# One instruction order from a table, and a ninth group on seven products, in a fused attention and feed-forward kernel

## The chip, the cores and the metric

The kernel runs on one core of a Trainium2 chip. The metric is the device time of one execution in microseconds (us). A core has engines that each run their instructions in order: TensorE (PE, the matrix engine), VectorE (DVE), ScalarE (ACT), GpSimd (POOL) and SyncE (SP, which mostly starts DMAs). They wait for each other by semaphores. Matrix products land in PSUM banks, which DVE and ACT read.

## What is computed

```python
B, H, S, D = 8, 8, 512, 64        # x: (B, H, S, D), state: (B, H, 32, D)
scale = 1.0 / np.sqrt(D)
scores = scale * x @ state^T ; a = softmax(scores)
xread = a @ state                  # tokens read from the states
scores2 = scale * state @ x^T ; a2 = softmax(scores2)
sread = a2 @ x                     # states read from the tokens
attn = concat([xread, sread], axis=2)          # 544 rows for each b and h
x = attn.transpose(0, 2, 1, 3).reshape(4352, 512)
h = x @ w_in                       # 512 -> 2048
out = (h * clip(h + 3, 0, 6) / 6) @ w_out      # 2048 -> 512, float32
```

## The kernel before

The rows of tokens of a batch are the attention weights times the states, so the kernel multiplies the states into w_in first: for every batch it makes W' = states x w_in (`wprime`, L660), in four chunks c of 512 of the 2048 inner columns, and takes the attention weights `aT` straight into the feed-forward product. Work goes in 144 steps n: 16 for each of the 8 batches, 16 for the rows of states of all batches. A step has a first product (`first`, `first_grouped`: `ps_h<-aT,wp`), a gate on ACT (L1204, L1374) and DVE (L1206, L1377), a split of the result in a high and a low half of 16 bits, `g_hi` and `g_lo`, and a second product (`second`, `second_grouped`) that adds into accumulators `acc0` to `acc3`. A product of two split operands is three terms: hi hi, hi lo, lo hi (`product`, L1133 is its matmul). The split is near (ACT makes hi, DVE lo, L422 and L423) or far (ACT hi, DVE minus hi, and an accumulating DMA of POOL adds the number itself, L449, L450, L452).

Batches from `HALF_FROM` = 2 on work in 16-bit floats; before them the operands are 32 bits wide. A batch with a number in `SEVEN` is grouped: its 512 tokens are two groups q of 256 with 8 steps each, and a step has 256 inner columns. Bit q of `SEVEN[b]` says that group q makes its second product by a scheme of Strassen's kind: 2 x 2 blocks with seven products of 128-blocks in place of eight. For that DVE makes two sums of gated blocks (L1215: one of 256 elements, one of 384), the weights have mixed forms T (`mixed_weights`), and the seven results are added up at the end of the group (L1280). A batch with 0 there has 16 steps of 512 tokens and 128 inner columns.

The order of the work is a plan. Each operation is recorded by `add` (through `T` for PE, `V` DVE, `S_` ACT, `P_` POOL, `Q` for DMAs of SP) with an engine, an expected cost, a rank, what it depends on and which buffers (slots) it takes. `order` places them by expected times: the first 566 of a table `OPENING`, then always an operation that could start soonest, by rank among those that start about equally soon. Tables of steps (`PLANS`, `FETCH`, `PAIRED_AT`, `MIXED_AT`, `CONVERTED`, `WPRIME_AT`) and others (`FAR`, `BEHIND`) set the ranks. `issue` runs the operations in that order, so the order of every engine is fixed when the program is built; in the opening it puts idle matmuls into expected gaps of PE (L1834).

Side work for a later batch is laid between the steps: DMAs that load x and the state, transposes of x on DVE (L806), scores of the states over the tokens and their softmax (`states`: row maximum L997, exps L1001), a move of those weights into another layout by a DVE transpose and 16 DMAs on SP (`weights_moved`, L1060), the states' read (`tokens_read`: PE L1089, with a scaling L1098 and a copy L1064 of the result on DVE), and the weights' split forms (L531, `converted`, `w_in_paired`).

The rows of states come last. Their two accumulators of 128 x 512 are emptied at the end of `second`: one by DVE (L1445), the last by ACT (L1442), and each is stored by a DMA of SP (L1460).

Of the kernel before, what the change touches and what calls it, by code (L numbers as in the profile page):

```python
# [46 lines left out]
SEVEN = [0, 0, 0, 0, 3, 3, 3, 3]  # L47
PAIRED = 3
WPRIME_AT = [1, -3, -2, -3]
BY_PAIRS = False  # L50
PAIRED_AT = [44, 30, 49, 30]
MIXED_AT = [44, 42, 50, 44, 48, 55, 48, 65]
CONVERTED = [19, 21, 29, 29, 30, 33, 33, 30, 31, 39, 36, 37, 34, 44, 37, 43]
EXTRA_FROM = 70
PLANS = [[1, -6, 16, 12, 5, -4, 4, 7], [-4, 5, 2, 14, 8, 5, 6, 8], [-12, -6, -11, 10, 5, 4, -5, 7], [-5, 4, 10, 9, 6, -10, 27, 9], [-9, -1, 9, 20, -1, -3, -5, 2], [-6, 2, -1, 24, 5, 13, -5, 21], [-5, 0, 12, 10, 6, 2, 18, 6]]
FETCH = [[4, 4], [19, 16], [26, 26], [39, 42], [61, 50], [69, 73], [95, 74]]
STATES_AT = 25
MAXIMA_AT = 25
WEIGHTS_AT = 20
FAR = [0, 0, 1, 1, 3, 4, 4, 1]  # L60
BEHIND = [1.0, 0.75, 1.75]
ADDED = 2.3
SLOWER = 1.18
EVICTED = (2, 3, 4, 5, 6, 7)
OPENING_ROWS = 566
SQUEEZE = 0.3
URGED = [34, 2.0]
PLAIN = 1
STATES = 121
# [3 lines left out]
OPENING = """  # L73
# [16 lines left out]
class Plan:  # L90
# [51 lines left out]
    def order(self):  # L142
        opening = [self.told[int(n)] for n in OPENING.split()[:OPENING_ROWS] if self.told[int(n)] is not None]
        n_ops = len(self.ops)
        held = {}
# [3 lines left out]
        self.home = {}  # L149
        waits = [len(op[4]) for op in self.ops]  # L150
        heirs = [[] for _ in range(n_ops)]
        for n, op in enumerate(self.ops):
            for d in op[4]:
                heirs[d].append(n)
        ready = [0.0] * n_ops
        open_ops = {e: set() for e in "TVSPQ"}
        for n in range(n_ops):
            if not waits[n]:
                open_ops[self.ops[n][0]].add(n)
# [4 lines left out]
        row, self.start, self.took = [], [0.0] * n_ops, [0.0] * n_ops  # L164
        placed = set()
        while len(row) < n_ops:
            best = None
            while opening and opening[0] in placed:
                opening.pop(0)
            told = opening[0] if opening and not waits[opening[0]] else None  # L170
            if told is not None:
                e = self.ops[told][0]
                t = max(clock[e], ready[told])
                for x in sorted(self.extra & open_ops[e], key=lambda x: (self.ops[x][2], x)) if len(row) > EXTRA_FROM else ():
                    at = max(clock[e], ready[x])
                    room = all(slot in held or any(f[0] <= at for f in free[slot[0]]) for slot in self.ops[x][5])
                    if room and at + self.ops[x][1] <= t + (1.0 if e == "Q" else SQUEEZE):
                        told = x
                        break
            more = opening and told is None and any(self.extra & s for s in open_ops.values())  # L180
            for e, numbers in open_ops.items():
                if told is not None:
                    numbers = {told} & numbers
                elif more:
                    numbers = self.extra & numbers
                can = []
                for n in numbers:
                    need = {}
                    for slot in self.ops[n][5]:
                        if slot not in held:  # L190
                            need[slot[0]] = need.get(slot[0], 0) + 1
                    if any(len(free[tag]) < k for tag, k in need.items()):
                        continue
                    t = max(clock[e], ready[n])
                    for tag, k in need.items():
                        t = max(t, sorted(free[tag])[k - 1][0])
                    if e == "Q":
                        t = max(t, min(flying))
                    can.append((t, self.ops[n][2], n))
                if not can:  # L200
                    continue
                soon = min(can)[0]
                t, rank, n = min(
                    (c for c in can if c[0] <= soon + (0.8 if c[1] <= 0.0 else 0.3)),
                    key=lambda c: c[1:],
                )
                if best is None or soon < best[0]:
                    best = (soon, t, n, e)
            if best is None:
                stuck = [self.ops[n][3].__name__ for s in open_ops.values() for n in s]  # L210
                raise RuntimeError(f"the plan is stuck: {stuck[:20]}; held: {[s for s in held if left[s]]}")
            _, t, n, e = best
            _, cost, _, _, _, slots, size = self.ops[n]
            if e == "T" and t < self.WARM:
                cost *= 2
            self.took[n] = cost
            new = [slot for slot in slots if slot not in held]
            for tag in dict.fromkeys(slot[0] for slot in new):
# [1646 lines left out]
```

## Time and profile before

| | us |
|---|---|
| median of 3 runs | 607.17 |
| lowest, highest | 606.9, 610.45 |
| the profiled execution's own time | 607.82 |
| its span, first to last instruction | 605.9 |
| PE, DVE, ACT, POOL busy | 594.2, 482.6, 387.4, 82.0 |

The granted clock of TensorE is 1.0 of full speed, its 2.4 GHz level, in practically the whole span. Busy time counts an engine's instructions; the span is one execution on the chip. An engine that is busy for less than the span waits somewhere, but only a wait of the engine that sets the end costs time. A matmul of 256 columns is one instruction, and so is one of 512; a step's time on PE is that of its matmuls together.

### The profile page before, as it was taken

The numbers are of one execution on the slowest core, as the hardware profiler recorded it, in microseconds if no ns is written. First come the engines' busy times: TensorE is split into PE (matmuls) and PEld (weight loads), VectorE is DVE, ScalarE is ACT, GpSimd is POOL, SyncE is SP. The second block draws the span as 40 slices with busy tenths as digits, with TensorE's granted clock in tenths as the row PEclk, the third lists the DMA queues.
The fourth block names the chain that finished last, engine by engine and source line by source line (L and its number), as shares of the span: only waits on it lengthen the run. The fifth ranks groups of instructions, "written<-read, shape, count | busy, mean of one in ns | idle before, by whom it ended". The sixth has DMA issues, their size and how long they took to land.

```text
span 605.9 us, 12698 instructions
## 1 busy us (share of the span) xinstructions
PE 594.2 (98%) x5041; PEld 424.6 (70%) x5041; DVE 482.6 (80%) x870; ACT 387.4 (64%) x633; POOL 82.0 (14%) x102
## 2 busy tenths in 40 slices
PE   8999999999999999999999999999999999999996
PEld 6577778778554444444468877888778878888763
DVE  6989997588899985598689887987879888788432
ACT  5988888887576765574565656475645566464432
POOL 2000000113231212220102011212121210000000
PEclk9999999999999999999999999999999999999999
DMA  8999152978691477993368594935497451211101
GB/s 288 376 196 326 48 127 36 204 141 141 117 244 18 75 95 110 185 173 48 43 123 134 77 142 52 160 48 67 85 141 116 83 63 18 51 16 16 70 2 35
DMA packets 148987, 67.99 MB, mean 112 GB/s; under 512 B 124864, under 2 KB 137792, under 8 KB 148800
## 3 DMA queue, kind: packets, MB, share of 16 engines
q1 hardware_dynamic: 135824, 45.95, 32.0%
q0 software_dynamic: 12960, 21.17, 25.5%
q8 instruction: 39, 0.64, 0.5%
q14 instruction: 20, 0.16, 0.1%
q10 hardware_dynamic: 144, 0.07, 0.0%
HBM read 33.41 MB, written 8.91 MB: 70 GB/s over the span
## 4 chain that ended last, share of the span: by engine, by line
PE 82%; DMA 6%; DVE 4%; SPq 4%; ACT 1%; issue 1%; DVEq 0%; ACTq 0%
PE acc L1133 48%; PE ps_h L1133 27%; PE both L660 4%; SPq L1060 3%; DMA early<-in_moe_w_in_dram 2%; DMA tmp<-in_state_dram 2%; DMA raw<-raw 1%; PE ps_h L1089 1%; SPq L646 1%; PE ps_h L660 1%; DVE wp L423 1%; DMA raw<-in_x_dram 1%; PE ps_h L1834 1%; ACT wp L422 0%; DMA out_dram<-ot 0%
## 5 line engine op out<-in xcount | busy, mean ns | idle before, releaser
L1133 PE MATMUL ps_h<-aT,wp 128*128 128x256 f16 (+2 forms) x1050 | 164.5, 303 | 0.0
L1133 PEld LDWEIGHTS <-g_hi 128*128 128x128 f16 x1216 | 117.9, 98 | 49.0 <-issue 4.7
L1133 PE MATMUL acc<-w,g_hi 128*128 128x256 f16 (+1 forms) x704 | 133.8, 321 | 0.0
L1133 PEld LDWEIGHTS <-wp 128*128 128x128 f16 x960 | 93.6, 98 | 32.1 <-issue 0.8
L1204 ACT ACTIVATE G<-ps_h,three 128x512 f32<-128x512 f32 x64 | 49.7, 777 | 49.8 <-PE ps_h L1133 46.6
L1133 PEld LDWEIGHTS <-g_lo 128*128 128x128 f16 x608 | 58.2, 98 | 27.6 <-issue 3.8
L1133 PE MATMUL acc<-w,g_lo 128*128 128x256 f16 (+1 forms) x352 | 75.6, 321 | 0.2 <-DVE g_lo L423 0.2
L1133 PE MATMUL acc<-T,g_hi 128*128 128x256 f16 x512 | 69.3, 273 | 0.0
L1374 ACT ACTIVATE g<-ps_h,three 128x512 f32<-128x512 f32 x64 | 47.0, 734 | 33.5 <-PE ps_h L1133 31.9
L452 POOL DMA_DIRECT2D g_lo<-G x42 | 36.8, 876 | 219.4 <-DVE g_lo L450 68.9
L1215 DVE TENSOR_TENSOR G<-G 128x256 f32<-128x256 f32 (+1 forms) x128 | 62.9, 491 | 4.3
L1377 DVE SCALAR_TENSOR_TENSOR g<-g,ps_h 128x512 f32<-128x512 f32 x64 | 43.5, 681 | 21.1 <-ACT g L1374 20.4
L449 ACT CAST g_hi<-G 128x896 f16<-128x896 f32 x42 | 39.3, 935 | 26.1 <-DVE G L1215 24.0
L1206 DVE SCALAR_TENSOR_TENSOR G<-G,ps_h 128x512 f32<-128x512 f32 x64 | 43.7, 683 | 11.5 <-ACT G L1204 11.2
L1133 PE MATMUL acc<-w_out_hi,g_hi 128*128 128x512 f32 x124 | 49.5, 400 | 0.0
L1133 PE MATMUL acc<-w_out_hi,g_lo 128*128 128x512 f32 x124 | 48.3, 390 | 0.0
L1133 PE MATMUL acc<-w_out_lo,g_hi 128*128 128x512 f32 x124 | 48.3, 390 | 0.0
L422 ACT ACTIVATE g_hi<-G 128x896 f16<-128x896 f32 (+1 forms) x38 | 27.5, 723 | 19.4 <-DVE G L1215 12.1
L1133 PE MATMUL acc<-T,g_lo 128*128 128x256 f16 x256 | 38.7, 273 | 0.0
L423 DVE SCALAR_TENSOR_TENSOR wp<-both,wp 128x512 f16<-128x512 f32 x36 | 24.0, 689 | 15.7 <-ACT wp L422 15.5
L423 DVE SCALAR_TENSOR_TENSOR g_lo<-G,g_hi 128x896 f16<-128x896 f32 (+1 forms) x38 | 30.6, 806 | 7.3 <-ACT g_hi L422 7.1
L1599 POOL DMA_DIRECT2D w_out_hi<-w_out_lo x16 | 13.9, 867 | 137.2 <-DVE room L1509 90.4
(196 smaller groups left out, 876.3 us busy)
## 6 DMA issues: line engine op xcount, KB each, us to landing
g_lo<-G POOLq DMA_DIRECT2D x42, 224.0 KB, 4.1
xb<-in_x_dram SPq DMA_DIRECT2D x32, 256.0 KB, 5.1
raw<-in_x_dram SPq DMA_DIRECT2D x112, 64.0 KB, 3.3
early<-in_moe_w_in_dram SPq DMA_DIRECT2D x5, 1023.0 KB, 9.4
w_out_hi<-w_out_lo POOLq DMA_DIRECT2D x16, 256.0 KB, 4.1
out_dram<-ot SPq DMA_DIRECT2D x4, 1024.0 KB, 5.2
raw<-w POOLq DMA_DIRECT2D x16, 256.0 KB, 4.1
out_dram<-ot SPq DMA_DIRECT2D x8, 512.0 KB, 2.8
```

The source lines that it names most:

```text
L422: S(cost, rank, lambda: nc.scalar.mul(hi(), src(), by()), [*reads, *keys], first_, after)
L423: V_(cost, rank, lambda: nc.vector.scalar_tensor_tensor(lo(), src(), by(), hi() if hi().dtype == F16 else hi().bitcast(F32), op0=ALU.mult, ...
L449: S(cost, rank, lambda: nc.scalar.copy(hi(), src()), reads, [writes[0]], after)
L452: P__(0.87, rank, lambda: nc.gpsimd.dma_start(lo(), src(), accum_op=ALU.add), reads, [writes[1]], (), size)
L660: nc.tensor.matmul(out[q // 2 if by_pairs else u][at * NS : (at + 1) * NS, :], (made["stT", b] if left is None else left)[rows, cols], mov ...
L1060: nc.sync.dma_start(dst[:, :, q], src[:, :, c])
L1133: nc.tensor.matmul(ps, l, r, start=start and k == 0, stop=stop and k == len(pairs) - 1)
L1204: S_(0.73, rank, lambda: nc.scalar.activation(g(), h(), AF.Relu, bias=three_of(G_SCALE / 4), scale=scales["gate7"]()), [ps, ("scale", "gat ...
L1206: V(0.63, rank, lambda: nc.vector.scalar_tensor_tensor(g(), g(), 6.0 * G_SCALE / 4, h(), op0=ALU.min, op1=ALU.mult), [ps], [key])
L1215: V(cost, rank, lambda out=out, one=one, other=other, op=op: nc.vector.tensor_tensor(blocks(*out), blocks(*one), blocks(*other), op=op), [ ...
L1374: S_(cost + (0.12 if scaled else 0.05), rank, lambda: nc.scalar.activation(g(), bank(ps)[:, :width], AF.Relu, bias=three_of(by), scale=sca ...
L1377: V(cost, rank, lambda: nc.vector.scalar_tensor_tensor(g(), g(), 6.0 * by, bank(ps)[:, :width], op0=ALU.min, op1=ALU.mult), [ps], [g_key])
```

## The change

`SEVEN` gets a 2 for batch 3: that batch is now grouped (two groups of 256 tokens), and its second group works with seven products. Groups with seven products are nine in place of eight.

`order` no longer chooses. A table `ORDER` holds all 2928 operations in the order in which they are recorded and issued; the loop only assigns buffers and works out expected start times, for the idle matmuls. The tables of steps and the constants of expected costs change with it. The table was found by a search over expected times.

The last accumulator of the rows of states is emptied in two halves of 256 columns, the first by ACT and the second by DVE, and stored in two DMAs, one started by ACT, one by SP.

```diff
-SEVEN = [0, 0, 0, 0, 3, 3, 3, 3]
+SEVEN = [0, 0, 0, 2, 3, 3, 3, 3]
-WPRIME_AT = [1, -3, -2, -3]
+WPRIME_AT = [1, -3, -2, -2]
-PAIRED_AT = [44, 30, 49, 30]
-MIXED_AT = [44, 42, 50, 44, 48, 55, 48, 65]
+PAIRED_AT = [37, 34, 32, 40]
+MIXED_AT = [51, 39, 54, 40, 52, 54, 50, 52]
...
-FETCH = [[4, 4], [19, 16], [26, 26], [39, 42], [61, 50], [69, 73], [95, 74]]
-STATES_AT = 25
+FETCH = [[4, 4], [19, 16], [26, 28], [37, 39], [60, 50], [70, 74], [91, 75]]
+STATES_AT = 16
...
-WEIGHTS_AT = 20
-FAR = [0, 0, 1, 1, 3, 4, 4, 1]
-BEHIND = [1.0, 0.75, 1.75]
+WEIGHTS_AT = 21
+FAR = [0, 0, 1, 3, 3, 4, 3, 2]
+BEHIND = [0.0, 0.5, 1.5]
...
-STATES = 121
+STATES = 117
...
-OPENING = """
-1 0 2 5 3 4 24 79 27 30 92 34 28 31 36 29 35 32 6 44 33 37 43 38 39 45 41 40 46 49 47 42 56 48 50 25 51 61 11 57 52
...
+ORDER = """
+1 0 5 2 3 4 24 79 92 27 34 6 28 29 11 35 30 37 36 31 32 44 38 43 33 39 45 41 40 46 49 47 42 56 48 50 25 51 61 57 52 26
...
-        while len(row) < n_ops:
-            best = None
...
+        row = [int(n) for n in ORDER.split()]
+        assert sorted(row) == list(range(n_ops))
...
+        for n in row:
+            e, cost, _, _, deps, slots, size = self.ops[n]
+            assert deps <= placed
+            t = clock[e]
+            for d in deps:
+                t = max(t, self.start[d] + self.took[d] if e == "T" == self.ops[d][0] else done[d])
...
+            elif b == B and j == nt - 1:
+                for k, (add, do) in enumerate(((S_, nc.scalar.mul), (V, nc.vector.tensor_scalar_mul))):
+                    es = slice(k * DO // 2, (k + 1) * DO // 2)
+                    add(0.42, rank, lambda j=j, acc=acc, es=es, do=do: do(ot()[:, j, es], bank(acc)[:, es], ends()),
+                        [acc, *end_keys], [(*ot_key, j, k)])
...
+                store = lambda queue, k, j=j, rows=rows, W=DO // 2: queue.dma_start(
+                    ov[rows, :, k * W : (k + 1) * W], ot()[:, j, k * W : (k + 1) * W])
+                S_(0.1, n + LAG, lambda store=store: store(nc.scalar, 0), [(*ot_key, j, 0)])
+                Q(n, 131.0, lambda store=store: store(nc.sync, 1), [(*ot_key, j, 1)])
```

The lines of the changed kernel stand 44 further down than before (55 in the last part). Three places show how the order moves; in each, the rows are those of DVE, first before, then after.

DVE when the first products of batch 2 are made ready (at 155 us in the profile before). `wp<-` is the low half of W', from the banks `ps_h` and `both`; `tmp<-raw` is the transpose of x that a DMA has brought to `raw`.

```order
L1601 SCALAR_TENSOR_TENSOR w_1645<-w_out_hi_536,room,w_1645 128x512
L423 SCALAR_TENSOR_TENSOR aT<-tmp,aT 128x1024
L806 STREAM_TRANSPOSE tmp<-raw 128x1024
L423 SCALAR_TENSOR_TENSOR wp<-ps_h,three,wp 128x512 x2
L423 SCALAR_TENSOR_TENSOR wp<-both,three,wp 128x512 x2
```

```order
L467 SCALAR_TENSOR_TENSOR aT<-tmp,aT 128x1024
L472 TENSOR_TENSOR g_lo<-g,g_hi 128x512
L1656 SCALAR_TENSOR_TENSOR w_1511<-w_out_hi_511,room,w_1511 128x512
L467 SCALAR_TENSOR_TENSOR wp<-ps_h,three,wp 128x512 x2
L850 STREAM_TRANSPOSE tmp<-raw 128x1024
L467 SCALAR_TENSOR_TENSOR wp<-both,three,wp 128x512
```

The transpose of x stood ahead of the splits out of `ps_h`; now it stands behind them and ahead of those out of `both`.

DVE at the beginning of batch 4 (at 302 us before). `nm` is the row maximum over the scores in `both`, `sr` and `sread_t` are copies out of the states' read.

```order
L1098 TENSOR_TENSOR sr<-ps_h,r_1972 128x128
L1064 COPY sread_t<-ps_h 128x128
L450 TENSOR_SCALAR g_lo<-g_hi 128x512
L997 TENSOR_REDUCE nm_2710<-both 128x2
L998 TENSOR_SCALAR nm_2710<-nm_2710 128x2
L955 STREAM_TRANSPOSE tmp<-both 128x1024
```

```order
L1001 STREAM_TRANSPOSE tmp<-tmp 128x1024
L1041 TENSOR_REDUCE nm_3458<-both 128x2
L1108 COPY sread_t<-ps_h 128x128
L1042 TENSOR_SCALAR nm_3458<-nm_3458 128x2
L467 SCALAR_TENSOR_TENSOR aT<-tmp,aT 128x1024
L1142 TENSOR_TENSOR sr<-ps_h,r_2872 128x128
L999 STREAM_TRANSPOSE tmp<-both 128x1024
L883 TENSOR_REDUCE s_3527<-tmp 128x32
```

The maximum stood behind both copies of the read; now it is ahead of both.

DVE in batch 6 where x of batch 7 is transposed (from 429 us before). Each `G<-G,ps_h` is one step's gate.

```order
L806 STREAM_TRANSPOSE tmp<-raw 128x1024
L423 SCALAR_TENSOR_TENSOR wp<-both,wp 128x512 x2
L1206 SCALAR_TENSOR_TENSOR G<-G,ps_h 128x512
L1215 TENSOR_TENSOR G<-G 128x256
L1215 TENSOR_TENSOR G<-G 128x3x128
L423 SCALAR_TENSOR_TENSOR g_lo<-G,g_hi 128x896
L1206 SCALAR_TENSOR_TENSOR G<-G,ps_h 128x512
L1215 TENSOR_TENSOR G<-G 128x256
L1215 TENSOR_TENSOR G<-G 128x3x128
L450 TENSOR_SCALAR g_lo<-g_hi 128x896
L806 STREAM_TRANSPOSE tmp<-raw 128x1024
```

```order
L850 STREAM_TRANSPOSE tmp<-raw 128x1024
L1250 SCALAR_TENSOR_TENSOR G<-G,ps_h 128x512
L1259 TENSOR_TENSOR G<-G 128x256
L1259 TENSOR_TENSOR G<-G 128x3x128
L467 SCALAR_TENSOR_TENSOR st_1615<-stT,room,st_1615 128x128
L850 STREAM_TRANSPOSE tmp<-raw 128x1024
```

Between the two transposes stood two steps' gates; now there is one. On PE, four first products stand between the first of the transposes and the states' read (`ps_h<-xb,raw`) before, and five after. On SP, the 16 moves (`raw<-raw`) for that read stood in one row; now a load of x (`xb<-in_x_dram`) stands behind the ninth.

## Rows read from the trace of the kernel before

**Rows 1.** Busy time of TensorE in the whole span, from the page.
```profile
PE 594.2 (98%) x5041; PEld 424.6 (70%) x5041; DVE 482.6 (80%) x870; ACT 387.4 (64%) x633; POOL 82.0 (14%) x102
```

**Rows 2.** Windows: start:end, length; busy us (instructions) of PE, PEld, DVE, ACT, POOL.
```profile
0.00:20.00 20.00, 17.99 (x177) 12.78 (x177) 14.00 (x37) 12.46 (x25) 3.57 (x12) 1.00 0.89 309
20.00:40.00 20.00, 18.41 (x99) 12.33 (x100) 16.07 (x33) 17.29 (x38) 0.00 (x0) 1.00 0.98 273
...
40.00:600.00 560.00, 556.94 (x4764) 399.28 (x4763) 451.74 (x801) 356.94 (x571) 78.38 (x90) 1.00 0.56 100
```

**Rows 3.** Waits of PE: what waited, on what; us, times, longest.
```profile
PE ps_h L1089 <- DMA raw<-raw: 1.4, 1, 1.4
PE ps_h L1133 <- DVE wp L423: 0.9, 1, 0.9
PE both L1039 <- DVE wp L428: 0.8, 1, 0.8
...
PE ps_h L1834 <- PEq L1849: 0.8, 1, 0.8
...
PE both L660 <- DVE G L1206: 0.4, 1, 0.4
```

**Rows 4.** The chain that ended last: start, us, what (matmuls in it).
```profile
24.66 12.41 DMA early<-in_moe_w_in_dram
...
163.34 1.31 PE ps_h L1133 x6
...
178.17 2.59 PE acc L1133 x12
...
322.25 1.31 PE ps_h L1133 x12
323.56 2.29 PE acc L1133 x21
...
439.63 6.19 DMA raw<-raw
```

**Rows 5.** Groups of DVE by form: count | busy, mean ns | idle before.
```profile
L1215 DVE TENSOR_TENSOR G<-G 128x384 f32<-128x384 f32 x64 | 35.7, 558 | 2.2
L1215 DVE TENSOR_TENSOR G<-G 128x256 f32<-128x256 f32 x64 | 27.2, 424 | 2.1
...
L1280 DVE TENSOR_TENSOR ot<-ot 128x512 f32<-128x512 f32 x24 | 16.4, 685 | 1.1 <-ACT ot L1241 0.8
```

**Rows 6.** Windows around batch 3's second group, and one early in batch 2.
```profile
266.00:300.00 34.00, 33.84 (x230) 14.56 (x229) 25.94 (x43) 18.80 (x28) 5.21 (x6) 1.00 0.49 72
...
240.00:306.00 66.00, 65.84 (x553) 29.84 (x552) 48.59 (x77) 36.94 (x60) 10.72 (x13) 1.00 0.69 119
...
160.00:180.00 20.00, 20.00 (x162) 12.03 (x161) 18.77 (x31) 13.58 (x24) 7.38 (x9) 1.00 0.95 188
```

**Rows 7.** Timeline of PE, ACT and SP's queue at the end; ACT's halves by form.
```profile
600.51 0.38 PE L1133 MATMUL acc<-w,g_lo 128*128 128x512 f16 x1
...
600.93 0.69 ACT L1442 ACTIVATE ot<-acc,three 128x512 f32<-128x512 f32 x1 [2.36 <-PE acc L1133]
...
601.06 1.29 SPq L1460 DMA_DIRECT2D out_dram<-ot  x2
...
L1241 ACT ACTIVATE ot<-acc,three 128x256 f32<-128x256 f32 x8 | 3.8, 474 | 0.0
```

**Rows 8.** Timeline of DVE near 155 us.
```profile
155.00 1.25 DVE L806 STREAM_TRANSPOSE tmp<-raw 128x1024 f32<-128x1024 f32 x1 [2.14 <-DMA raw<-in_x_dram]
156.17 1.37 DVE L423 SCALAR_TENSOR_TENSOR wp<-ps_h,three,wp 128x512 f16<-128x512 f32 x2
```

**Rows 9.** Timeline of DVE, then ACT, near 302 to 306 us.
```profile
302.12 1.19 DVE L997 TENSOR_REDUCE nm<-both 128x2 f32<-128x1024 f32 x1
...
306.10 0.68 ACT L1001 ACTIVATE tmp<-both,nm 128x512 f32<-128x512 f32 x1
```

**Rows 10.** Timeline of SP's queue near 430 us.
```profile
430.57 13.24 SPq L1060 DMA_DIRECT2D raw<-raw  x16
```

More of the change, by code (lines that the diff above doesn't have):

```diff
@@ L142, in order @@
     def order(self):
-        opening = [self.told[int(n)] for n in OPENING.split()[:OPENING_ROWS] if self.told[int(n)] is not None]
-        n_ops = len(self.ops)
-        held = {}
+        held, self.home = {}, {}
         left = {slot: len(users) for slot, users in self.users.items()}
@@ L148, in order @@
         free = {tag: [(0.0, i) for i in range(count)] for tag, count in self.slots.items()}
[L149 to L159, printed above, removed]
         clock = dict.fromkeys("TVSPQ", 0.0)
@@ L163, in order @@
         flying = [0.0] * 8
-        row, self.start, self.took = [], [0.0] * n_ops, [0.0] * n_ops
+        n_ops = len(self.ops)
+        done, self.start, self.took = [0.0] * n_ops, [0.0] * n_ops, [0.0] * n_ops
+        row = [int(n) for n in ORDER.split()]
+        assert sorted(row) == list(range(n_ops))
         placed = set()
-        while len(row) < n_ops:
-            best = None
[L168 to L216, printed above, removed]
@@ L222, in order @@
                 for slot, place in zip(mine, got):
+                    t = max(t, place[0])
                     held[slot] = place
                     self.home[slot] = place[1]
-            self.start[n] = t
+            if e == "Q":
+                t = max(t, min(flying))
+            if e == "T" and t < self.WARM:
+                cost *= 2
+            self.start[n], self.took[n] = t, cost
             clock[e] = t + cost
-            done = t + cost + self.AFTER[e]
+            end = t + cost + self.AFTER[e]
             if size and e == "P":
-                adding = done = max(t + ADDED, adding) + size + min(max(0.0, channel - t - ADDED), size)
+                end = max(t + 1.9, adding) + size + 0.5 * min(max(0.0, channel - t - 1.9), size) + 0.3
+                adding = end
             elif size:
-                channel = max(channel, t + 1.15) + size / self.transfer * (SLOWER if t > 30.0 else 1.0)
-                done = channel + (0.7 if n < self.first_loads else 0.9)
+                at = max(channel, t + 1.15, adding - 0.9 if size <= 200.0 else 0.0)
+                channel = at + size / self.transfer * (1.1 if 30.0 < t < 100.0 else 1.0)
+                end = channel + (0.7 if n < self.first_loads else 0.9) + 0.15
                 flying.remove(min(flying))
-                flying.append(done)
+                flying.append(end)
+            done[n] = end
             for slot in slots:
                 left[slot] -= 1
-                until[slot] = max(until[slot], done)
+                until[slot] = max(until[slot], end)
                 if not left[slot]:
                     free[slot[0]].append((until[slot], held[slot][1]))
-            open_ops[e].discard(n)
             for more_room in self.growing:
@@ L243, in order @@
                     more_room[1].discard(n)
-                    more_room[2] = max(more_room[2], done)
+                    more_room[2] = max(more_room[2], end)
                     if not more_room[1]:
                         free[more_room[0]].append((more_room[2], more_room[3]))
-            for h in heirs[n]:
-                own = e == "T" == self.ops[h][0]
-                ready[h] = max(ready[h], t + cost if own else done)
-                waits[h] -= 1
-                if not waits[h]:
-                    open_ops[self.ops[h][0]].add(h)
-            row.append(n)
             placed.add(n)
@@ L1440, in second @@
                     [acc], [(*ot_key, j)])
[L1441 removed]
+            elif b == B and j == nt - 1:
[3 more added lines that the diff above has]
+                        [acc, *end_keys], [(*ot_key, j, k)])
+            elif b < B and (j % 2 == 0 or b in EVICTED):
                 S_(0.62, rank, lambda j=j, acc=acc: nc.scalar.mul(ot()[:, j, :], bank(acc), ends()),
```

14 lines of the change are left out of this document (5 added, 9 removed), and 128 rows, old and new, of tables (OPENING, ORDER).

## The prediction

> **What bounds the kernel now.** I read the busy times first: TensorE (PE) works 594.2 of 605.9 us [rows 1]. Then the busy time by stretches, to see where the missing 11.7 us are: 2.0 in the first 20 us, 1.6 in the next 20, 3.1 between 40 and 600 [rows 2], and the rest, about 5.0, behind the last matmul. So two kinds of saving exist: columns taken off PE, and those 6.7 us of waits and the tail. No other engine can give anything by itself; VectorE (DVE), with 482.6 us busy, can only take something away. Third I read PE's waits: 1.4 for the blocks that SyncE's (SP's) DMAs move for the states' read, 0.9 and 0.8 for W' splits on DVE, 0.4 at a W' product, and 0.8 of its own start [rows 3]. Last the chain, for the steady price of a step: a first product takes 1.31 us, and a second product 2.59 with eight products and 2.29 with seven [rows 4].
>
> **Seven products in eight more steps.** Eight steps, those of batch 3's second group, go from 12 matmuls of 512 columns (2.59) to 21 of 256 (2.29): 8 x 0.30 = 2.40 us less on PE, which sets the end. Sixteen first products, all of batch 3, change from 6 matmuls of 512 to 12 of 256. The two rows show 1.31 for either form [rows 4], so I count nothing. The Trainium skill (TensorE: Matmul & The Clock Gate, Back-to-back issue gap) gives the gap between matmuls as columns / 2.4 GHz plus 2.5 ns, so 96 more matmuls would cost an estimated 0.24 us and this part would give 2.2 instead of 2.4; the rows above don't show this surcharge.
>
> The price is on DVE: each of the eight steps adds one sum of 384 elements and one of 256, 0.558 + 0.424, together 7.9 us; and four additions more into results, three of 512 elements at 0.685 and a smaller one, at most 2.7 [rows 5]. That is 10.6 us on an engine which is idle for 123 us of the span, off the path if it can be spread. Between 266 and 300 us, where batch 3's second group runs now, DVE is busy 25.9 of 34; over 240 to 306 it is 48.6 of 66 [rows 6]. With all of the 10.6 the longer stretch would be 59.2 of 63.6 (93%); between 160 and 180 it is busy 18.77 of 20 (94%) with PE at 20.00 [rows 6]. So I count nothing here, under the condition that the added work isn't bound to the short stretch (third rival).
>
> **The end.** Today the last matmul ends at 600.9, ScalarE (ACT) takes 0.69 for the last 128x512 eviction from 600.93, and SP issues the last two stores one behind the other, 1.29 for both from 601.06 [rows 7]. A 128x256 eviction takes 0.474 on ACT [rows 7], so the last one ends about 0.2 earlier. By the new order the accumulator before the last is complete six matmuls before the end, not three, so its store is issued some 0.65 earlier (three 512-column matmuls, a quarter of 2.59) and SP is free when its half is there. Nothing in the trace shows ACT issuing a store; between nothing (what follows a store sets the end anyway) and 0.6 (one of the two issues gone) I take 0.25, nearer to the eviction row.
>
> **The waits that the new order moves.** Four are named in PE's waits.
> At 155.6 PE waits 0.9 for W' splits. DVE, idle 2.14 for x to land, does the 1.25 us transpose of x first and then the splits [rows 8]. Now the ps_h splits stand ahead of that transpose, and a late x holds only the splits of the other banks: 0.93 gone.
> At 306 a W' product waits 0.43. The row maximum (1.19) stood on DVE behind two copies that wait for the states' read, so the two exps on ACT were late, the second at 306.10 with a gate in between [rows 9]. Now the maximum is ahead of both copies: 0.43 gone.
> At 445 the read waits 1.4. The 16 moves behind it could be issued by SP only at 430.57, when the first transpose of x of batch 7 had freed their buffer, and the issues took 13.24 us [rows 10]. Then 6.19 us of a DMA stand on the chain [rows 4]. Counted on PE, four first products stand between that transpose and the read before, five now: one more step, 1.31 + 2.29 = 3.6 us of cover for 1.4 us. Against it stand loads of x put among the moves on SP; one issue costs about 13.24 / 16 = 0.8, so three of them would use up the 2.2 that are left, and one stands there. Gone.
> At 39 the transposes for the weights wait 0.8 for a split that stood on DVE behind a rounding of w_in; the split is moved ahead, and PE has three more matmuls between. Gone.
> Together 0.93 + 0.43 + 1.37 + 0.82 = 3.55 us. I see no second wait close behind any of them: PE is busy 20.00 of 20 right after the one at 155 [rows 6], and between 40 and 600 us only 0.3 of its 3.1 idle stands elsewhere [rows 2, 3].
>
> **The opening** is re-ordered and its idle 2.0 + 1.6 less the 0.8 counted leaves 2.8, of which the first 0.8, the engine's start [rows 3], can't go. Bounds 2.0 better and 1.0 worse; I take 0.3 better, because the loads of the weights hold much of that stretch: the chain lies on one for 12.41 us [rows 4].
>
> **New waits.** The whole order is new, also where nothing waited. A fixed order keeps in-order engines waiting for whatever is later than the search expected. Bounds: nothing, and 5.0, a second set of waits as large as all that the old order lost behind 20 us (1.6 + 3.1, and a little for refilling). Nearest is the old order itself, which outside the named places lost only 0.3 in 560 us. For every second product I counted the PE work between a first product and the first matmul on its low half, in both orders, at the rows' prices: in batches 4 to 7 at least 7.3 us before and 10.2 now, so more slack. Below the smallest that the old order had outside the opening (6.5) it falls only at the end of batch 1, to 4.3 and 6.3 in two steps, from 8.9 and 10.9. I take 1.0.
>
> **Sum** against the profiled run's 607.82: −2.40 −0.25 −3.55 −0.30 +1.00 = −5.50, so 602.3. The median of the three runs is 0.65 below the profiled one: 601.7. One per cent, about what a measurement of this kernel can tell from no change, is 6.1 us; its lower bound is 601.1, close below the forecast.
>
> **Rivals.**
> First, only the arithmetic stays. For: an order fixed by expected times loses where DMAs land late, and two of the four waits hang on DMAs. Against: in the old order, too, the instructions of an engine were fixed when the kernel ran. Of the 3.55 all would come back elsewhere: 607.82 − 2.4 − 0.25 − 0.65 = 604.5.
> Second, the search takes nearly all waits behind 20 us. For: the cover above grew. 607.82 − 2.4 − 0.25 − 1.6 − 3.1 − 0.3 = 600.2, less 0.65 = 599.5; with an opening better by 1 more, 598.5.
> Third, slower: DVE becomes the bound in batch 3's second group. If the sums and the rest must be done where its steps run, DVE needs 25.9 + 10.6 = 36.5 us in a stretch that lasts 34 − 2.4 = 31.6 on PE. It decides once the work there exceeds 31.6; then PE waits 4.9, and the maximum, copies and splits for batch 4 queue behind it for another wait like the 1.4 at 445: 602.3 + 4.9 + 1.4 = 608.6, less 0.65 = 608.0. Against: the high halves of steps 57 to 62, which are made of those sums, are wanted only 13 to 18 us of PE work after their first products, three steps and more, so the sums can be spread.
> That the change doesn't do what it says has no room: the order of PE holds 96 matmuls of 512 columns fewer in the second product and 168 of 256 more.
>
> **How the numbers follow.** Forecast 601.7 (600.3 to 603.3): 0.50. First rival 604.5: 0.22. Second 599.5: 0.22. Third 608.0: 0.06. The range 598.4 to 605.6 leaves out the third and the tails of the other rivals. Faster by over 1% (below 601.1): the second rival and somewhat over a third of the forecast, 0.40. Slower by over 1% (above 613.2): 0.02. Within: 0.58.
>
> **What would show it.** PE busy about 591.8; windows of batch 3's second group at PE 100% with DVE at 90% or more; no wait of PE for raw<-raw; no wait of the first product for splits near 155; a last eviction of 0.47. Wrong would be the forecast if PE's waits after 20 us sum to over 3 us (first rival), if DVE's sums release PE between 260 and 300 (third), or if PE's busy time doesn't fall by 2.4.

## The result and the profile after

The changed kernel takes 601.93 us (median of 6 runs, 600.98 to 603.94); the kernel before takes 607.71 beside it. The ratio of the two is 0.990, its 95% interval 0.987 to 0.993. The profiled execution takes 602.23 with a span of 600.4. The forecast was 601.7.

Busy time from the page, and windows (start:end, length, then busy us of PE, PEld, DVE, ACT, POOL, the granted clock, the DMA share, GB/s), beside [rows 1, 2]:

```profile
PE 591.5 (99%) x5208; PEld 441.4 (74%) x5208; DVE 481.1 (80%) x891; ACT 386.9 (64%) x635; POOL 86.5 (14%) x108
```

```profile
0.00:20.00 20.00, 18.00 (x176) 13.22 (x176) 14.22 (x37) 12.48 (x26) 3.03 (x12) 1.00 0.86 298
20.00:40.00 20.00, 19.98 (x109) 13.85 (x109) 17.51 (x34) 18.62 (x38) 0.00 (x0) 1.00 0.98 297
...
40.00:595.00 555.00, 552.65 (x4923) 414.14 (x4922) 448.54 (x820) 355.31 (x572) 83.50 (x96) 1.00 0.58 102
```

PE's busy time fell by 2.7 us, from 594.2. Its idle time stays 2.0 in the first 20 us, falls from 1.6 to 0.0 in the next 20, and is 2.35 from 40 us to shortly ahead of the last matmul, where it was 3.06. PE's waits (what waited, on what; us, times, longest), beside [rows 3]:

```profile
PE ps_h L1133 <- DMA raw<-raw: 1.8, 1, 1.8
...
PE ps_h L1177 <- ACT wp L466: 0.3, 1, 0.3
...
PE ps_h L1177 <- DVE wp L467: 0.2, 1, 0.2
```

Of the four named waits, those at 39, 306 and 445 us are gone. The one at the first products of batch 2, 0.9, is down to 0.3 + 0.2. But a wait for `raw<-raw`, the 16 moves behind a states' read, is there again: it is now the read of batch 4, not of batch 6, and it is 1.8, not 1.4. Here are SP's queue and PE at that place, beside [rows 10]:

```profile
281.47 6.24 SPq L1104 DMA_DIRECT2D raw<-raw  x8
287.81 0.54 SPq L1281 DMA_DIRECT2D out_dram<-ot  x1
288.39 5.45 SPq L1104 DMA_DIRECT2D raw<-raw  x6
293.88 0.60 SPq L672 DMA_DIRECT2D xb<-in_x_dram  x1
294.53 1.25 SPq L1104 DMA_DIRECT2D raw<-raw  x2
```

```profile
298.64 0.30 PE L1133 MATMUL ps_h<-xb,raw 128*32 128x64 f32 x2
300.74 1.32 PE L1133 MATMUL ps_h<-xb,raw 128*32 128x64 f32 x62 [1.81 <-DMA raw<-raw]
```

Fourteen of the moves are issued with a store between them, then comes a load of x (`xb<-in_x_dram`, 256 KB), and then the last two moves. The first of them lands at 300.70, 6.17 us after its issue, and PE was ready for it at 298.9; the second takes 5.7. The moves issued just ahead of the load took 1.9 to 2.0. An accumulating DMA of POOL (224 KB) had begun 0.3 us ahead of the two:

```profile
294.23 0.86 POOL L496 DMA_DIRECT2D g_lo<-G  x1 [5.88 <-DVE g_lo L494]
```

The end, on PE, ACT, DVE and SP in turn, beside [rows 7]:

```profile
595.48 0.38 PE L1177 MATMUL acc<-w,g_lo 128*128 128x512 f16 x1
...
595.89 0.47 ACT L1488 ACTIVATE ot<-acc,three 128x256 f32<-128x256 f32 x1 [2.94 <-PE acc L1177]
596.40 0.65 ACTq L1512 DMA_DIRECT2D out_dram<-ot  x1
...
596.40 0.48 DVE L1488 TENSOR_SCALAR ot<-acc,three 128x256 f32<-128x256 f32 x1 [1.05 <-ACT ot L1488]
...
596.91 0.58 SPq L1512 DMA_DIRECT2D out_dram<-ot  x1
```

From the last matmul's end (595.86) to the end of the span are 4.54 us; before, 5.03 (600.89 to 605.92). DVE's half did not run beside ACT's: it stood idle for 1.05 us and began when ACT had ended, at 596.36. So the last eviction ended 0.3 us later behind the last matmul than before (1.02, was 0.73), not earlier.

The place that [rows 8] showed, on DVE:

```profile
157.90 1.25 DVE L850 STREAM_TRANSPOSE tmp<-raw 128x1024 f32<-128x1024 f32 x1 [1.77 <-DMA raw<-in_x_dram]
159.06 0.71 DVE L467 SCALAR_TENSOR_TENSOR wp<-both,three,wp 128x512 f16<-128x512 f32 x1
```

The transpose of x still waits for x, and a split of `both` stands behind it. The window of [rows 6] from 240 to 306 us:

```profile
240.00:306.00 66.00, 64.15 (x656) 44.19 (x655) 51.30 (x91) 39.68 (x61) 13.90 (x16) 1.00 0.81 135
```

DVE is busy 51.3 of 66 us there, 2.7 more than before, and PE idle 1.85, nearly all of it the read's wait. Within it, where the second group of batch 3 runs now:

```profile
260.00:300.00 40.00, 38.89 (x370) 27.95 (x368) 34.84 (x63) 22.92 (x33) 6.90 (x8) 1.00 0.93 157
```

DVE is busy 87% there, a little under the 90% that was forecast.

### The profile page after: what moved, and what is told of

It is laid out like the page before. It is cut to its first block, busy times and chain, and to the rows that moved or that the text cites. A ratio compares the mean times of both kernels' runs of the same rounds, so it can differ in the third digit from the quotient of the medians.

```text
span 600.4 us, 13141 instructions
## 1 busy us (share of the span) xinstructions
PE 591.5 (99%) x5208; PEld 441.4 (74%) x5208; DVE 481.1 (80%) x891; ACT 386.9 (64%) x635; POOL 86.5 (14%) x108
## 4 chain that ended last, share of the span: by engine, by line
PE 87%; SPq 5%; DVE 3%; DMA 3%; issue 1%; ACT 1%
PE acc L1177 50%; PE ps_h L1177 29%; PE both L704 4%; SPq L1104 3%; DMA raw<-raw 2%; PE ps_h L1133 1%; SPq L690 1%; PE acc L1455 1%; DMA raw<-in_x_dram 1%; SPq L672 1%; DMA st_raw<-in_state_dram 0%; PE ps_h L704 0%; DVE w_in L575 0%; PE both L925 0%; PE acc L861 0%
## 5 line engine op out<-in xcount | busy, mean ns | idle before, releaser
L1177 PEld LDWEIGHTS <-wp 128*128 128x128 f16 x1056 | 102.7, 98 | 26.7 <-issue 1.8
L1248 ACT ACTIVATE G<-ps_h,three 128x512 f32<-128x512 f32 x80 | 62.2, 777 | 57.8 <-PE ps_h L1177 42.2
L1177 PE MATMUL acc<-T,g_hi 128*128 128x256 f16 x576 | 89.9, 273 | 0.0
L493 ACT CAST g_hi<-G 128x896 f16<-128x896 f32 (+1 forms) x52 | 47.2, 907 | 34.1 <-DVE G L1259 23.9
L1250 DVE SCALAR_TENSOR_TENSOR G<-G,ps_h 128x512 f32<-128x512 f32 x80 | 54.5, 682 | 13.9 <-ACT G L1248 13.5
L467 DVE SCALAR_TENSOR_TENSOR g_lo<-G,g_hi 128x896 f16<-128x896 f32 (+2 forms) x44 | 36.1, 820 | 29.9 <-ACT g_hi L466 22.1
L1177 PE MATMUL acc<-T,g_lo 128*128 128x256 f16 x288 | 59.3, 273 | 0.0
L466 ACT ACTIVATE g_hi<-G 128x896 f16<-128x896 f32 (+2 forms) x44 | 32.2, 731 | 26.7 <-PE acc L1177 16.7
L1418 ACT ACTIVATE g<-ps_h,three 128x512 f32<-128x512 f32 x48 | 34.3, 717 | 14.2 <-PE ps_h L1177 13.6
L1421 DVE SCALAR_TENSOR_TENSOR g<-g,ps_h 128x512 f32<-128x512 f32 x48 | 32.5, 682 | 8.7 <-ACT g L1418 8.4
```

The lines of the kernel that those rows point to most:

```text
L466: S(cost, rank, lambda: nc.scalar.mul(hi(), src(), by()), [*reads, *keys], first_, after)
L467: V_(cost, rank, lambda: nc.vector.scalar_tensor_tensor(lo(), src(), by(), hi() if hi().dtype == F16 else hi().bitcast(F32), op0=ALU.mult, ...
L493: S(cost, rank, lambda: nc.scalar.copy(hi(), src()), reads, [writes[0]], after)
L1177: nc.tensor.matmul(ps, l, r, start=start and k == 0, stop=stop and k == len(pairs) - 1)
L1248: S_(0.73, rank, lambda: nc.scalar.activation(g(), h(), AF.Relu, bias=three_of(G_SCALE / 4), scale=scales["gate7"]()), [ps, ("scale", "gat ...
L1250: V(0.63, rank, lambda: nc.vector.scalar_tensor_tensor(g(), g(), 6.0 * G_SCALE / 4, h(), op0=ALU.min, op1=ALU.mult), [ps], [key])
```

## The experiments

The kernels ran in three groups, those of a group on one chip beside the kernel before (608.2, 608.92 and 607.73 us in the three). The changed kernel itself ran only in the third; in the first two, "above the changed kernel" means above the 601.93 of the result. In the third it took 603.61, so such differences are uncertain by one to two us, and the argument rests on the profiles. Line numbers are the changed kernel's if nothing else is said. Where the edit is a move in the table of the order, the diff names the operation by its number there.

### Eight products again

```diff
-SEVEN = [0, 0, 0, 2, 3, 3, 3, 3]
+SEVEN = [0, 0, 0, 4, 3, 3, 3, 3]
```
Batch 3 stays grouped, with eight products in both groups; 54 operations that then don't exist are out of the table, and the rest keeps its order.

> The changed kernel with eight products in batch 3's second group again, in the order of the table (operations that eight products don't need are taken out of it). Theory A, the seven products are worth their matmuls: PE has 2.4 us more, time up by 2.4 to 604.3. Rival B, part of the 2.4 went into the new wait of 1.8 at the read of the states, which is set by DMAs and not by PE: PE comes to the read 2.4 later, the wait vanishes, time up by only 0.6 to 602.5. Rival C, the sums on DVE cost what the products saved: no change or faster, at most 601.9.

Measured: 604.37 us, ratio 0.9935 (0.9914 to 0.9957), 2.4 above the changed kernel. Busy time from its page:

```profile
PE 594.2 (98%) x5136; PEld 433.8 (72%) x5136; DVE 470.9 (78%) x871; ACT 382.4 (63%) x633; POOL 86.3 (14%) x108
```

PE has 2.7 us more than in the changed kernel, and the time agrees with theory A. But what rival B describes happened too. The two reads, of batch 3 and of batch 4:

```profile
256.07 1.21 PE L1131 MATMUL ps_h<-xb,raw 128*32 128x64 f32 x62 [0.57 <-issue]
...
303.17 1.10 PE L1131 MATMUL ps_h<-xb,raw 128*32 128x64 f32 x64
```

The 1.8 wait of batch 4's read is gone. In its place stand 0.6 at the read before it, waits of 0.5 and 0.5 in the opening, and some of 0.2 to 0.3, so that PE's idle time as a whole, 9.1 us, is that of the changed kernel (8.9). That the time rose by just what PE's work did is therefore in part chance: against the kernel below that hardly waits at batch 4's read either (0.2; 600.65, same group), it is 3.7. DVE's 10 us less in this kernel bring nothing, against C. Beside the kernel before (608.2) this kernel is 3.8 faster: that much the order and the end give without the seven products in batch 3.

### The old way of ordering, with nine groups

```diff
-SEVEN = [0, 0, 0, 0, 3, 3, 3, 3]
+SEVEN = [0, 0, 0, 2, 3, 3, 3, 3]
```
This is the kernel before; `PAIRED_AT`, `MIXED_AT` and `CONVERTED` are those of the changed kernel.

> The kernel before, with its order chosen by expected times as it was, and nine groups on seven products (the steps at which the mixed and paired weights are made are those of the changed kernel, since batch 3 needs them earlier). Theory A, the seven products carry their 2.4 us in any order and the rest of the gain is the table's: 607.7 - 2.4 = 605.3. Rival B, the old way of ordering pays for the added sums and the earlier weights with new waits that are as large: 607.7 or above. Rival C, the nine groups are all of the gain: 602.

Measured: 622.1 us, ratio 1.0218 (1.0186 to 1.025). Its costliest waits, and the worst stretch (line numbers of the kernel before):

```profile
PE acc L1133 <- DMA g_lo<-G: 4.0, 4, 2.1
PE ps_h L1107 <- DVE G L1206: 3.0, 1, 3.0
PE ps_h L1133 <- ACT aT L422: 2.8, 1, 2.8
```

```profile
300.00:320.00 20.00, 12.76 (x110) 8.62 (x108) 15.72 (x25) 9.04 (x14) 0.00 (x0) 0.91 0.22 39
```

PE is idle 7.2 of 20 us from 300 on, where batch 4 begins: it waits for gates and weights that stand late on DVE and ACT. B holds, far beyond its number. The other tables of this kernel were not searched again for the new work, and `FAR` is the old one too (DVE is busy 495.6 us, 13 more than before). So this shows what nine groups cost in an order that wasn't made for them, and not the best that the old way could do.

### More sums

```diff
                 V(cost, rank, lambda out=out, one=one, other=other, op=op: [nc.vector.tensor_tensor(
                     blocks(*out), blocks(*one), blocks(*other), op=op)
+                    for _ in range(4 if b == 3 and op == ALU.subtract else 1)], [], [key])
```

> The changed kernel with the first sum of each step of batch 3's second group (256 elements, 0.42 us on DVE) done four times in place of once, with the same result: 8 x 3 x 0.42 = 10.1 us more on DVE, as much again as the seven products brought there. Theory A, DVE has room in that stretch but not for this (it is busy 34.8 of the 40 us from 260 to 300): about half of it, 3 to 6 us, comes out as waits of PE: 605 to 608. Rival B, the order has so much slack that the sums spread: under 0.5 us. Rival C, DVE is the bound there already: all of it, 612.

Measured: 606.32 us, ratio 0.9961 (0.9942 to 0.998): 4.4 above the changed kernel. The window of batch 3's second group and the waits of PE that are new:

```profile
260.00:300.00 40.00, 35.40 (x307) 25.23 (x304) 37.41 (x76) 20.48 (x32) 6.03 (x7) 1.00 0.86 146
```

```profile
PE acc L1177 <- ACT g_hi L493: 2.4, 2, 1.4
PE both L704 <- DVE wp L467: 1.4, 3, 1.1
```

DVE is busy 37.4 of 40 us (34.8 in the changed kernel), and PE idle 4.6 (1.1). Theory A holds: 10.1 us of DVE work become 3.5 us of idle PE in this window and, between the groups, 4.4 us of time. The third rival's mechanism exists; the sums that the change added stayed on the near side of its point.

### The transpose of x ahead of the splits

In the table, operation 857 (the transpose) goes from behind 741 to ahead of 739 (739 and 741 are the two splits out of `ps_h`):
```diff
-... 739 ... 741 ... 857 ...
+... 857 739 ... 741 ...
```

> The changed kernel with one instruction of DVE put back: the transpose of x of batch 3 stands ahead of the two splits of W' out of ps_h again, as in the kernel before. Theory, a late x holds what stands behind it on DVE: in the changed kernel x lands at 157.9, so the splits would end near 160 and the first product that starts at 156.0 would wait some 3.5 to 4 us; the two later waits there (0.3 and 0.2) go into it; time up by 3 to 3.5, to about 605. Rival, this place was no gain of the order (x is late wherever its transpose stands, and PE has other work): no change, 601.9.

Measured: 607.45 us, ratio 0.9979 (0.996 to 0.9998): 5.5 above the changed kernel, more than the theory said. DVE, then PE's first product of batch 2:

```profile
158.47 1.25 DVE L850 STREAM_TRANSPOSE tmp<-raw 128x1024 f32<-128x1024 f32 x1 [3.19 <-DMA raw<-in_x_dram]
159.64 1.37 DVE L467 SCALAR_TENSOR_TENSOR wp<-ps_h,three,wp 128x512 f16<-128x512 f32 x2
```

```profile
160.40 2.42 PE L1177 MATMUL ps_h<-aU,wp 128*128 128x512 f32 x6 [3.12 <-DVE wp L467]
```

The wait is 3.1, as the theory has it. The rest is in the windows behind it (the clock is the third number from the end of a row):

```profile
160.00:162.00 2.00, 1.60 (x5) 1.32 (x6) 1.73 (x4) 0.00 (x0) 0.00 (x0) 0.76 0.00 0
162.00:164.00 2.00, 2.00 (x6) 1.52 (x6) 0.36 (x1) 1.08 (x2) 0.00 (x0) 0.50 0.00 0
164.00:166.00 2.00, 2.00 (x9) 1.61 (x8) 2.00 (x4) 1.50 (x4) 0.00 (x0) 0.89 0.00 0
166.00:168.00 2.00, 2.00 (x10) 1.08 (x9) 1.72 (x3) 1.77 (x4) 1.05 (x2) 1.00 0.02 4
```

The granted clock falls to 0.50, the 1.2 GHz level, after the idle stretch, and is back at 1.00 at 166. The three rows below 1.00 lack 0.48 + 1.00 + 0.22 = 1.7 us of work at full speed. Busy time of PE is 594.0, 2.5 us more for the same matmuls, so 0.8 of that lies elsewhere. The wait for `raw<-raw` near 300 is gone here, but a wait of 1.4 for a load of the state (`st_raw<-in_state_dram`) stands in its place.

### The load of x ahead of the moves, twice

In the table, operation 882 (the load) goes ahead of 1320, the first move:
```diff
-1320 1319 ... 1322 ... 882 ... 1316 ... 1313
+882 1320 1319 ... 1322 ... 1316 ... 1313
```

> The changed kernel with one DMA moved on SP: the last load of x of batch 4 goes ahead of all 16 moves for the states' read, where it stood behind the fourteenth. In the changed kernel PE waits 1.8 us at that read. Theory A, the load between the moves holds up the last two (0.6 us of issue and 256 KB ahead of them): the wait falls below 0.3 and the time by 1.5 to 1.8, to about 600.3. Rival B, the moves land late because POOL's accumulating DMA began 0.3 us ahead of them (at 294.2, as at 439.3 in the kernel before, where a move issued 0.3 us later took 6.19 us): the wait stays at 1.2 to 1.8, the time at 601.3 to 601.9. Rival C, the load delays the first move as much as it now delays the last: 601.9.

Measured: 600.65 us, ratio 0.9871 (0.9847 to 0.9895); 0.2 of the wait is left in its profile. In the third group it ran beside the changed kernel:

> The load of x ahead of the moves once more, beside the changed kernel. Theory: 1.0 to 1.5 us below the changed kernel of this call, and the executions lie closer together. Rival, the two kernels' medians came from different chips: no difference.

> The changed kernel itself, on the same chip as the three beside it. Median 601.9 within 1 us; PE's wait at the read of the states near 300 us between 0.5 and 1.8 (it was 1.8 and, with the same order there, 0.5 in another run).

Measured there: 600.40 (ratio 0.9868, 0.9841 to 0.9894; 599.71 to 600.61) against 603.61 for the changed kernel (ratio 0.9911, 0.9885 to 0.9938; 600.36 to 604.04). So the gain was 3.2, more than expected, and both forecasts for the changed kernel missed: its median is 1.7 above 601.9, and its wait was 2.5. SP and then PE in the kernel with the load moved:

```profile
279.90 0.60 SPq L672 DMA_DIRECT2D xb<-in_x_dram  x1
281.99 6.42 SPq L1104 DMA_DIRECT2D raw<-raw  x8
288.52 0.55 SPq L1281 DMA_DIRECT2D out_dram<-ot  x1
289.11 6.73 SPq L1104 DMA_DIRECT2D raw<-raw  x8
...
299.12 1.10 PE L1133 MATMUL ps_h<-xb,raw 128*32 128x64 f32 x64
```

All sixteen moves are issued by 295.84, and the read runs at 299.12 without a wait. Theory A's number holds, and C falls: the first move starts 0.5 later and it costs nothing. But A alone doesn't explain the wait. The last two moves in seven profiles (all times in us):

| kernel | load just ahead of them | POOL's DMA begins | the two are issued | and land after |
|---|---|---|---|---|
| changed | yes | 294.23 | 294.53, 295.16 | 6.2, 5.7 |
| changed, third group | yes | 293.83 | 294.14, 294.78 | 6.8, 6.4 |
| whole end (below) | yes | 293.53 | 293.03, 293.67 | 4.0, 5.0 |
| eight products | yes | 289.44, 297.00 | 294.24, 294.87 | 3.0, 2.6 |
| more sums | yes | 292.14, 301.24 | 298.42, 299.05 | 3.1, 2.6 |
| load ahead of the moves | no | 294.67 | 294.55, 295.20 | 3.6, 4.3 |
| the same, third group | no | 295.26 | 294.58, 295.23 | 3.5, 3.3 |

With the load ahead of them and no DMA of POOL begun close by they land after 2.6 to 3.1; with POOL's and without the load after 3.3 to 4.3; with both, and POOL's begun first, after 5.7 to 6.8. With the load alone they are there before PE comes (by 297.5 in the kernel with eight products, where PE was ready at 298.9 in the changed kernel). So B names the larger part and A the smaller, and A is right about the cure. No run moves POOL's DMA alone, so this is read from the traces and not tested. In the changed kernel of the same group the wait was 2.5 and drew the clock after it:

```profile
301.03 2.17 PE L1133 MATMUL ps_h<-xb,raw 128*32 128x64 f32 x62 [2.49 <-DMA raw<-raw]
```

```profile
300.00:302.00 2.00, 0.97 (x31) 0.97 (x35) 0.69 (x1) 0.67 (x1) 0.00 (x0) 0.77 0.05 7
302.00:304.00 2.00, 2.00 (x48) 1.58 (x40) 0.76 (x3) 0.00 (x0) 0.00 (x0) 0.50 0.00 0
304.00:306.00 2.00, 2.00 (x18) 1.71 (x17) 0.93 (x2) 1.79 (x5) 0.00 (x0) 0.88 0.03 8
```

The 62 small matmuls of the read take 2.17 us, not the 1.32 of the first profile, and PE's busy time is 592.8 in place of 591.5. The rows below 1.00 lack 0.46 + 1.00 + 0.24 = 1.7 us of work at full speed, so 0.4 of that is made up elsewhere. The wait and the lower clock are 2.5 + 1.7 = 4.2 us together, and the two spans differ by 3.6 (602.2 and 598.6). The wait was 1.8 in the first profile, 2.5 in this one, and 0.5 in the profile of the kernel with the whole end, whose order is the same there: the two moves land at a time that changes from run to run with what they meet. This fits that the changed kernel's runs lie 3 to 4 us apart and those of this kernel within 1.3.

### The end: whole, and in two banks

The first kernel undoes the halves:
```diff
-            elif b == B and j == nt - 1:
-                for k, (add, do) in enumerate(((S_, nc.scalar.mul), (V, nc.vector.tensor_scalar_mul))):
...
+            elif (j % 2 == 0 or b in EVICTED) if b < B else j == nt - 1:
```

> The changed kernel with the last accumulator emptied whole by ACT and stored by one DMA of SP, as before. Theory A, the halves save because the last transfer is half as large (landing 2.4 to 2.6 us after its issue, not 2.9): time from the last matmul to the end of the span goes from 4.5 back to 5.0, time up by 0.4 to 602.3. Rival B, the halves save nothing, since the second eviction starts only when the first has ended: the stretch stays at 4.5, and the gain came from the accumulator before the last being complete earlier, which stays in this kernel: 601.9.

Measured: 602.09 us, ratio 0.9894 (0.9871 to 0.9917), no difference that the runs can tell. ACT and SP at its end:

```profile
593.71 0.69 ACT L1486 ACTIVATE ot<-acc,three 128x512 f32<-128x512 f32 x1 [2.94 <-PE acc L1177]
...
594.42 0.58 SPq L1504 DMA_DIRECT2D out_dram<-ot  x1
```

The last matmul ends 0.04 ahead of ACT's eviction, at 593.67, and the span (598.6) 4.93 later, against 4.54 with halves. So the profile (of the fastest execution, 600.33) shows Theory A's 0.4, below what the medians resolve. The landing of a half takes 2.4 to 2.6 us after its issue and that of the whole 2.9, in both kernels' traces. But the store of the second half is issued 1.05 after the last matmul and that of the whole 0.75, so the shorter landing gives 0.2 of the 0.4; the other 0.2 is not explained.

The second gives the last accumulator two PSUM banks, on top of the moved load:
```diff
+                if b == B and js.stop == nt * P:
+                    for k, to in enumerate((acc, ("acc3", seg))):
+                        es = slice(k * DO // 2, (k + 1) * DO // 2)
+                        product(bank(to)[:, es], [((hi[:, js], lo[:, js]), [t[:, es] for t in w])], start, stop, h)
+                    return
```

> The kernel with the load ahead of the moves (600.65), and the last accumulator of the states' rows in two PSUM banks, 256 columns in each (its matmuls are halves, twice as many). In the changed kernel DVE's half was taken only when ACT's half was done (0.5 us later); a second reader of one bank waits for the first. Theory A: the halves are taken side by side, SP's store starts 0.5 earlier and the time falls by 0.3 to 0.5, to about 600.2. Rival B, the end hangs on ACT's store, whose issue takes 0.65: no change, 600.65.

Measured: 602.92 us, ratio 0.9902 (0.9878 to 0.9927), 2.3 above the load alone, though that ran in another group and the two intervals just overlap. DVE's half, and a wait that is new:

```profile
596.34 0.48 DVE L1493 TENSOR_SCALAR ot<-acc,three 128x256 f32<-128x256 f32 x1 [0.56 <-PE acc L1177]
...
PE acc L1177 <- ACT ot L1285: 1.6, 1, 1.6
```

DVE's half now follows PE and not ACT, and SP's store starts 0.56 us after the last matmul, not 1.05. But the span ends only 4.41 after it (4.54): most of the half microsecond doesn't reach the end, and SP's half lands 2.7 after its issue here, not 2.4. And PE's first matmul into the second bank waits 1.6 for ACT to empty it after batch 7. With `acc2` in place of `acc3`:

> The load ahead of the moves and the last accumulator in two PSUM banks, the second now the bank of acc2, which is emptied ahead of acc3 at the end of batch 7 (with acc3 PE waited 1.6 for ACT's eviction). Theory A, that wait is gone and the end is 0.15 shorter (4.4 us behind the last matmul, not 4.55): 0.1 to 0.2 below the kernel with the load alone. Rival B, acc2 is late as well: 0.5 to 1.5 above it.

Measured: 601.25 us, ratio 0.9881 (0.9857 to 0.9906), against 600.40 with the load alone in the same group; the wait is 0.7, as rival B has it, and the span ends 4.40 after the last matmul. No gain.

### The transpose of x behind all four splits

Operation 857 goes behind 743, the last of the four, on top of the two banks and the moved load:
```diff
-... 857 ... 745 ... 743 ...
+... 745 ... 743 857 ...
```

> The same with one more move: the transpose of x of batch 3 on DVE behind all four splits of W' of batch 2 (it stood between the first two and the last two). In the changed kernel PE waits 0.3 and 0.2 there. Theory A: both waits vanish, time down by another 0.4 to 0.5, to 599.7. Rival B, x comes too late for what is made of it and the wait returns there: 600.2 or above.

Measured: 602.18 us, ratio 0.9891 (0.9865 to 0.9917), beside 602.92 without it. PE's two waits for splits near 160 are not in its waits. They are hardly there without the move either: from 150 to 175 us PE is idle 0.1 us in both profiles, where it was 0.5 in the changed kernel's, with the same order there. So there was little to gain in this pair. From 40 to 260 us PE is idle 1.1 us, where it was 0.4 without the move; the most of it, 0.95, stands at the states' read near 255 (0.3). The intervals overlap; it stays open whether this move gains anything.

### The old opening

The first 360 operations stand in the order of the kernel before, with the moved load (the second half of the states' load stays where the table has it). The table `OPENING` of the kernel before has 400 entries, not 566, so nearly all of it is put back.
```diff
-1 0 5 2 3 4 24 79 92 27 34 6 28 29 ...
+1 0 2 5 3 4 24 79 27 30 92 34 28 31 ...
```

> The kernel with the load ahead of the moves, and its first 360 operations (about the first 50 us) in the order that the kernel before had; only the second half of the load of the states for their scales stays where the table has it. Theory A, the table's order of the opening took 1.6 us of waits out of the first 40 us (3.6 to 2.0 us of idle PE): idle 3.4 to 3.8 there, time up by 1.5. Rival B, the opening hangs on the loads, which this kernel issues nearly as the changed one: no change.

Measured: 601.29 us, ratio 0.9885 (0.986 to 0.991), against 600.40. Windows of the opening, and the waits that are back:

```profile
0.00:20.00 20.00, 17.78 (x176) 13.50 (x177) 13.52 (x37) 11.80 (x25) 3.59 (x12) 1.00 0.89 308
20.00:40.00 20.00, 19.20 (x105) 12.99 (x105) 17.18 (x34) 18.30 (x39) 0.00 (x0) 1.00 0.98 280
```

```profile
PE acc L1455 <- DVE g L1421: 0.8, 1, 0.8
...
PE ps_h L964 <- POOL w_in L953: 0.7, 1, 0.7
```

PE is idle 3.0 us in the first 40, against 2.1 with the table's opening: theory A, at 0.9 in place of 1.5. The loads of w_in (`early`, 1023 KB) land 9.4 us after their issue here, as in the kernel before, and 5.9 in the changed kernel, where SP issues them ahead of the wide loads of w_out. The wait at 39 us is not back, so its end isn't explained by the order of the opening alone.

## Why the prediction was right, point by point

**Seven products**, −2.40: measured 2.7 in PE's busy time, and 2.4 in time when they are taken out again, this last in part by chance. The surcharge that the Trainium skill (TensorE: Matmul & The Clock Gate, Back-to-back issue gap) gives would have left 2.2. I wrote that the rows don't show it, and this was misread: the second products do, 2.59 / 12 = 216 ns for 512 columns and 2.29 / 21 = 109 ns for 256, so two halves take about 2 ns more than a whole, in agreement with the Trainium skill. For 96 matmuls that is 0.2 us, less than these times can tell, and why PE's busy time fell by 2.7 stays open.

**DVE's side**, 0 under a condition: held. The condition was real, since 10.1 us more cost 3.5 to 4.4. But DVE is busy 78% of the longer stretch, not the 93% that I worked out. The added work is what I counted: from 240 to 306 us DVE is busy 51.3 with it and 40.9 with eight products in the same order, 10.4 more. It is the rest that is lighter than the 48.6 of before: `FAR`, which decides which splits are far (and not their rank), sends more of batch 3's to POOL (nine in this window, three before), which takes some 2 us off DVE, and side work now stands outside of the window.

**The end**, −0.25: measured −0.49, and the reason that I gave falls. The second half of the eviction waits for the first, since both read one PSUM bank; with separate banks it doesn't wait. This agrees with the Trainium skill (PSUM — Partial Sum Buffer, PSUM bank collisions raise a hardware error), by which two engines may not access one bank in the same partitions at once. The halves save about 0.4, of which a shorter last transfer explains 0.2; the remaining 0.1 is what the earlier completion of the other accumulator can have given, which wasn't tried alone.

**The four waits**, −3.55: −3.06 by the profile. At 155 us the mechanism was right (put back, it costs 3.1 of wait), and so was the remark that a late x holds the other splits: that is the 0.5 that stayed (0.1 to 0.5 in other profiles of this order). At 306 and 445 the waits are gone; that they went for the reasons given was not tried. For the one at 39 us my reason is open.

**The opening**, −0.30: −0.76 besides the wait at 39 us (3.60 to 2.02, less 0.82). The step that was mis-sized said that the loads hold the stretch and the order doesn't; the order of the loads themselves was part of the table, and they land 3.5 us sooner.

**New waits**, +1.00: +1.81, all of it one wait. I said that PE would not wait for `raw<-raw`. I had counted the load of x among the moves of batch 6's read, by its issue alone (0.8), and found cover enough there. I hadn't looked at the same pattern for batch 4's, where the load stands ahead of the last two moves and POOL's DMA beside them: there they took some 4 us longer to land than the moves before them. And 1.81 is one execution's number: with the same order the wait was 0.5 in another, and 2.5 with 1.7 of lower clock in a third.

These make −2.74 − 0.49 − 3.06 − 0.76 + 1.81 = −5.2; the remaining 0.3 are small waits between 40 and 600 us that are no longer there. The sum was −5.50 and the profiled runs differ by 5.59. So the total is right partly by luck: the gains that I took too small (0.3, 0.2 and 0.5 us, and the 0.3 that I hadn't counted) make up for a gain taken too large (0.5) and a loss taken too small (0.8). Which executions were measured was luck as well: in the third group the same kernel's median was 603.61, nearer to the first rival's 604.5 than to the forecast.

Of the rivals, the first happened in part (1.8 + 0.5 of the 3.55 came back as waits, but the other terms made up for it), the second is nearly reached by the kernel with the moved load, the fastest of all (600.4 and 600.7, against its 599.5), and the third's mechanism showed only with twice the sums.

## What to carry to other kernels

An order found on expected times is as good as its times for DMAs: the one large wait that was left hung on two small transfers that a large load had been put ahead of and that met a large transfer of POOL, and moving that load to where SP had nothing to do took 1.3 to 3.2 us off. When work is moved onto an engine with room, double it once: that the doubled work costs a third to a half of its length tells how near the edge the first portion is. And the two halves of a split eviction run side by side only with two banks; here that gave 0.1 at the end, and the second bank's release came too late for PE.

## What was not expected of the hardware

A wait of PE can cost more than its length. With PE idle for 1.81 us (the changed kernel at 300 us), 1.63 (the kernel with two banks, at 558) or 1.37 (before, at 445) the granted clock stayed at 1.00, the 2.4 GHz level; after 2.49 and after 3.12 us of idle it was at 0.50, 1.2 GHz, in the window from 302 to 304 and from 162 to 164. By the windows' clock this took 1.7 us of work at full speed each time. The length alone doesn't decide: in the old order with nine groups PE was idle for 2.98 us, and the clock stayed.

```profile
389.58 0.33 PE L1107 MATMUL ps_h<-ident,sr 128*128 128x128 f32 x1 [2.98 <-DVE G L1206]
...
390.00:392.00 2.00, 2.00 (x81) 1.07 (x69) 1.80 (x3) 1.68 (x3) 0.00 (x0) 1.00 1.26 176
```

A move of 32 KB within SBUF lands 2.6 us after its issue in the median of the changed kernel; the two behind the load and beside POOL's DMA landed after 6.2 and 5.7.
